# Attention into mixture of experts on one core: single steps of a written-out plan get offsets, work moves between VectorE and GpSimd, and all engines get a new order

## The chip, the cores and the metric

The kernel runs on one core of one Trainium2 chip. The metric is the device time of one execution in microseconds (us). PE is the matrix engine TensorE, DVE is VectorE, ACT is ScalarE, POOL is GpSimd, SP the engine that issues most DMAs.

## The reference

Inputs: q, k, v of 4 batches, 8 heads, 576 positions, 64 columns, and the weights of 8 experts. First an approximate attention with 32 landmarks a head, then an expert layer on its 2304 x 512 result.

```python
q_lm = q.reshape(B, H, m, S // m, D).mean(axis=3)        # m = 32, S // m = 18
k_lm = k.reshape(B, H, m, S // m, D).mean(axis=3)
A = sm(q, k_lm)                                          # sm: softmax of scaled products
Bm = sm(q_lm, k_lm)
C = sm(q_lm, k)
Z = Bm.transpose(0, 1, 3, 2) / (norm1 * norminf + 1e-06)
for _ in range(6):
    Z = 2 * Z - Z @ Bm @ Z
x = A @ Z @ C @ v
expert_idx = argmax(x @ w_gate); gate_w = softmax of it at that expert
h = maximum(x @ w1[e], 0); y = h @ w2[e]                 # each row by its own expert, up to a capacity
out = gate_w * y
```

## The kernel before

Heads are stacked on partitions in two groups of 64 columns. For each batch `b` the work is cut into streams, Python generators that yield one `Step` (an engine, a cost, what it depends on) ahead of the instructions that it issues:

- `loads`: q, k and v by DMA. `landmarks`: sums over 18 positions into `lmq` and `lmk`, in four pieces (q and k, each in two groups `g`). A letter in `CFG["lm"]` says who sums a piece: V is VectorE in one instruction, G is GpSimd in five (through `tr`), H is half and half.
- `chain`: Bm (`bp`), its softmax (`BB`), then `bbp` and six rounds `pp` on TensorE, each followed by an addition `PQ` on VectorE, and `Wd`. Batches 2 and 3 go through one chain together.
- `cpath` a = 0, 1: the products `psC` (256 and 320 columns), their maximum (L565), the bias (L567), the exponential `Cx` on ScalarE, the transposes `ctp` and `ctq`. `cval`: `cvp`, C times v.
- `apath` a = 0, 1: the products `psA`, then in `AW` a transpose, maximum, subtraction (L673), exponential, sum, product (L683) and a transpose into `AT` (L686). `CFG["aw"]` says whether VectorE or GpSimd does the subtraction and the product.
- `route`: `mtp` and its copy `MT` (what the expert layer needs of a batch), `gp`, `ltp`, `glg`; a copy `ei` of the expert's number goes to SP, which loads that expert's weights `w1` (four pieces, `w1load`) and `w2` (eight pieces, `wload`).

The expert layer assumes that a batch uses one expert and has a slow path, not run here, for the rest. A key is a batch's turn in it (0, 1, 2; on this path the last batch is written as zeros). The attention result isn't formed: `gps` is MT times w1, split in two parts `gh` and `gl` of reduced precision (L931, L933); A is split likewise into `ah` and `al` (L948, L951, engine by `CFG["al"]`). A hidden block is six products `hps` (L972) for one of 8 pieces `fc` of the hidden layer and one half `c` of the positions, then ScalarE and VectorE or GpSimd (by `CFG["rx"]`) turn it into `hx`. w2 is split into `wh` (ScalarE, L891) and `wl` (L897, VectorE or GpSimd by `CFG["lo"]`). An output tile is a sum over the 8 pieces, `ybank` or `yps` (L1031, L1036), scaled into `yo` and stored. Until the first output tile TensorE fills planned idle time with products of zeros (L1094).

`weave` is the planner, run when the program is built. It keeps a clock for each engine, takes from all ready steps those that could start soonest, and of those within a small window (`look`) the one with the lowest priority number. On TensorE a change of kind (reduced-precision blocks against the others) adds `sw` to the number. The order that comes out is each engine's program: every engine works its own list in order, and waits where something isn't there.

Of the kernel before, what the change touches and what calls it, by code (L numbers as in the profile page):

```python
# [14 lines left out]
ALU = mybir.AluOpType  # L15
# [3 lines left out]
class Step:  # L19
    def __init__(self, eng, cost, deps=(), order=(), name=None, res=None, nres=1, keep=False, free=None, prev=True, start=0, prio=None,  # L20
# [8 lines left out]
    sw=4000,  # L29
    sc='AAAV',  # L30
    rx='GGVVGVVVVVGGVGVGVGVVVGGGGGVGVGVGGGVVVGGVGVVGVVVG',
    look=0.05,
    tg='tfftfttffftfttfffffttfff',
    ce='AVAAAVAA',
    pa='ffsfffsf',
    aw='GVGGVGVVGVGGGGVV',
    ye='AAAVAAAAAVAVVAVA',
    lm='VVHVGGVVGVGGVVGV',
    al='VGGVVV',
    lo='VGVVGVVVGGGGGGGGGGGVVGVV',  # L40
    pr=[
# [4 lines left out]
    ],  # L46
    fr=[
        [2182, -3175, -6151, 655, -1689, 10070],
        [-3174, -3941, 2917, 6070, -3108, 5793],
        [-15, -4918, 3590, -371, -3463, -1305],  # L50
    ],
    sp=[-5732, -1101, 1345],
    ah=[-2564, -629, 3615, -5343, -3536, -3510],
    rl=[-3503, -3810, 5069],
    ev=[-3109, -45, -3647],
# [34 lines left out]
def weave(streams, banks, fill=None):  # L90
# [9 lines left out]
    def enable(s):  # L100
        step = s[2]
        for d in (*step.deps, *step.order):
            if d not in ev:
                wait.setdefault(d, []).append(s)
                return
        lag = step.start + HIN[step.eng]
        s[4] = max([0] + [ev[d] + lag for d in step.deps] + ([s[3] + lag] if step.prev and s[3] else []))
        s[5] = s[0] if step.prio is None else step.prio
        ready.append(s)

    def advance(s):
        s[2] = next(s[1], None)
        if s[2] is not None:
            enable(s)
        while spawned:
            advance([s[0], spawned.pop(0), None, s[3], 0, 0])

    for prio, gen in streams:
        advance([prio, gen, None, 0, 0, 0])
# [64 lines left out]
def nystrom_moe(ctx: ExitStack, tc: tile.TileContext, q, k, v, vtail, wgate, w1, w2, out, cap):  # L184
# [157 lines left out]
    def landmarks(b):  # L342
        lmt[b] = dict(q=None, k=None)
        for g in range(2):
            for nm in "qk":
# [9 lines left out]
                if e == "V":  # L355
                    parts = ((2, 3), (3, 4)) if b == 0 and g and nm == "k" else ((2 * g, 2 * g + 2),)
                    for i, (j0, j1) in enumerate(parts):
                        last = i + 1 == len(parts)
                        yield Step("V", 720 if j1 - j0 == 1 else 1290, deps=[f"ld{b}{nm}{j}" for j in range(j0, j1)], order=order,
                                   prev=False, name=f"lm{b}{g}{nm}" if last else None)  # L360
                        nc.vector.tensor_reduce(out=lm()[:, j0:j1, :], axis=AX.X, op=ALU.add,
                                                in_=st[b][nm][:, j0:j1, :].rearrange("p y (m t) -> p y m t", t=L))
                elif e == "P":
                    p = Step("P", 1450, deps=ld, order=order, prev=False, res="f", keep=True, kind="T")
# [3 lines left out]
                    for i in range(3):  # L368
                        if i:
                            yield Step("P", 1450, kind="T")  # L370
                        for t in range(6 * i, 6 * i + 6):
                            nc.tensor.matmul(ps, lhsT=ident, rhs=x[:, :, :, t], start=(t == 0), stop=(t == L - 1))
                    yield V(130, free=p, name=f"lm{b}{g}{nm}")
                    nc.vector.tensor_copy(lm()[:, 2 * g:2 * g + 2, :], ps)
                else:
                    j0, n = 2 * g, 2
                    if e == "H":
                        yield Step("V", 720, deps=ld[:1], order=order, prev=False, name=f"lv{b}{g}{nm}")
                        nc.vector.tensor_reduce(out=lm()[:, j0, :], axis=AX.X, op=ALU.add,
                                                in_=st[b][nm][:, j0, :].rearrange("p (m t) -> p m t", t=L))  # L380
                        j0, n = j0 + 1, 1
                    yield Step("G", 1300 if n == 2 else 700, deps=ld[2 - n:], order=order + ([f"lmg{b - 1}"] if b else []), prev=False)
# [55 lines left out]
    def V(c, **kw):  # L438
        return Step("V", c, **kw)

    def chain(*bs):
# [8 lines left out]
        def C(one, both):  # L450
            return both if two else one

        p = Step("P", C(222, 352), tag="a", deps=[x for b in bs for x in LM(b)],
# [54 lines left out]
        p = Step("P", C(356, 672), res="ch", keep=True)  # L508
# [10 lines left out]
        for it in range(6):  # L519
            last = it == 5  # L520
            p = Step("P", C(417, 770) if last else C(356, 672), res="ch", keep=True)
            yield p
            pp = pch.tile([128, n, 2, 32], F32, tag="ch", name="pp")
            for x in range(n):
                for j in range(4):
                    y = slice(32 * j, 32 * j + 32)
                    if last:
                        nc.tensor.matmul(pp[y, x, 1], lhsT=PQ[y, x, 0], rhs=PQ[y, x, 2], start=True, stop=False)
                        nc.tensor.matmul(pp[y, x, 1], lhsT=istk[y], rhs=PQ[y, x, 2], start=False, stop=True)
                    else:  # L530
                        nc.tensor.matmul(pp[y, x], lhsT=PQ[y, x, 0], rhs=PQ[y, x, 0:3:2], start=True, stop=True)  # L531
            if last:
                break
            yield V(C(200, 330), free=p)
            Pn = PQs[1 - it % 2][:, xs]
            nc.vector.tensor_tensor(Pn[:, :, 0:3:2, :], pp, PQ[:, :, 1:3, :], ALU.add)
            PQ = Pn
# [9 lines left out]
    def cpath(b, a):  # L547
# [18 lines left out]
        yield V(65)  # L566
        nc.vector.tensor_scalar(cs[:, 1, :, a], cs[:, 0, :, a], -SC1, None, op0=ALU.mult)  # L567
        Cx = at.tile([128, NG, n], F32, tag=f"C{a}", name="Cx")
        for x in range(NG):
            yield Step("A", 250 + n * 5 // 6, free=p if x else None, start=0 if x else 60,  # L570
                       name=[f"cx{b}{a}"] * x)
            nc.scalar.activation(Cx[:, x, :], t[:, x, :n], AF.Exp, bias=cs[:, 1, x, a:a + 1], scale=SC1,  # L572
                                 accum_out=sums[:, x, a:a + 1])
# [27 lines left out]
    def cjoin(b):  # L601
# [5 lines left out]
        yield Step("A", 300)  # L607
# [11 lines left out]
    def cval(b):  # L619
        for x in range(NG):  # L620
# [11 lines left out]
            def cvf(x=x, p=p, cvp=cvp):  # L632
                yield V(130, deps=[f"cg{b}"], order=[f"mt{b - 2}"] if b > 1 else ())
# [4 lines left out]
                yield V(130, free=p, name=[f"cv{b}{x}"] + [f"cv{b}"] * x)  # L638
                nc.vector.scalar_tensor_tensor(CV, cvp[:, 1, :], cf[:, 1, x, 1:2], CV, ALU.mult, ALU.add)
# [244 lines left out]
    def wsplit(b, key):  # L884
        st[b]["w"] = []
        for c in range(NFC):
# [12 lines left out]
            later(lo, e, 1280 if e == "G" else 610, name=f"ws{key}{c}", port=True)  # L899
# [268 lines left out]
```

## Time and profile before

| | |
|---|---|
| median of 3 runs | 188.54 us (187.79 to 188.80) |
| the profiled execution | 188.28 us |
| its span, first to last instruction | 186.6 us |
| busy: PE, DVE, ACT, POOL | 177.7, 108.2, 79.7, 78.6 us |

The span is what the profile shows; 1.68 us of the profiled execution lie around it. Instructions of different engines overlap, so busy times don't add up to the span.

### The profile page before, as it was taken

To read this page: it belongs to the slowest core of one execution; us is meant where nothing else is said; L and a number is where in the kernel's file an instruction comes from. 1 tells how busy PE (TensorE), PEld (TensorE's weight loads), DVE (VectorE), ACT (ScalarE), POOL (GpSimd) and SP (SyncE) were. 2 spreads that over 40 slices of the span, in tenths; PEclk is the share of its full clock that TensorE was granted. 3 is DMA by queue.
4 is the path that set the end of the run, shared out by engine and by line. 5 is a ranking of instruction groups with operands and counts; after the bars stand their busy time and mean duration, and the time that the engine had idled before them with its cause. 6 is when DMAs were issued, how large, how long until landed. Compare 5 with 4: busy or idle time off the path is not lost.

```text
span 186.6 us, 5484 instructions
## 1 busy us (share of the span) xinstructions
PE 177.7 (95%) x2191; PEld 136.0 (73%) x2199; DVE 108.2 (58%) x313; ACT 79.7 (43%) x202; POOL 78.6 (42%) x131
## 2 busy tenths in 40 slices
PE   7989987998999999999999999999999999999992
PEld 2435634667788788788778889688888899788891
DVE  2789999999899967884446767820002753211001
ACT  3026314976497402455496377501153976100020
POOL 7429996783037276505881256300025752100000
PEclk9999999999999999999999999999999999999998
DMA  5999969984631999284710059411115400011121
GB/s 187 401 407 405 378 233 349 335 287 134 218 134 21 394 366 359 75 265 166 226 56 4 4 180 362 137 32 56 56 56 154 134 0 0 4 32 56 63 84 41
DMA packets 17492, 31.95 MB, mean 171 GB/s; under 512 B 1520, under 2 KB 9584, under 8 KB 17456
## 3 DMA queue, kind: packets, MB, share of 16 engines
q1 hardware_dynamic: 17024, 31.07, 47.8%
q8 instruction: 19, 0.31, 0.7%
q10 hardware_dynamic: 432, 0.43, 0.7%
q14 instruction: 17, 0.14, 0.2%
HBM read 26.77 MB, written 4.72 MB: 169 GB/s over the span
## 4 chain that ended last, share of the span: by engine, by line
PE 71%; DVE 14%; DMA 6%; ACT 3%; issue 3%; POOL 2%; SPq 0%; DVEq 0%; ACTq 0%
PE yps L1031 19%; PE hps L972 17%; PE ybank L1031 16%; PE ybank L1036 6%; DMA qt<-in_q 3%; PE gps L691 3%; DMA w2t<-in_w 2%; PE pp L531 2%; DVE cs L565 2%; PE ctp L582 1%; PE cvp L629 1%; PE psC L559 1%; DVE gl L933 1%; PE psA L658 1%; ACT Cx L572 1%
## 5 line engine op out<-in xcount | busy, mean ns | idle before, releaser
L995 POOL TENSOR_TENSOR hx<-rr,hx 128x224 fp32r<-128x224 f32 (+2 forms) x38 | 22.3, 605 | 29.8 <-ACT hx L986 29.6
L1031 PE MATMUL yps<-wh,hx 128*128 128x512 f32 (+1 forms) x112 | 33.5, 375 | 0.0
L897 POOL TENSOR_TENSOR wl<-w2t,wh 128x512 fp32r<-128x512 f32 x14 | 17.8, 1286 | 31.6 <-ACT wh L891 30.0
L1031 PE MATMUL ybank<-wh,hx 128*128 128x512 f32 (+1 forms) x96 | 28.5, 371 | 0.0
L972 PE MATMUL hps<-ah,gh 128*128 128x288 f32 x80 | 25.2, 315 | 0.1
L1031 PEld LDWEIGHTS yps<-wh,hx 128*128 128x128 f32 x112 | 20.6, 188 | 4.2 <-issue 0.4
L972 PE MATMUL hps<-al,gh 128*128 128x288 f32 x80 | 23.6, 295 | 0.0
L972 PE MATMUL hps<-ah,gl 128*128 128x288 f32 x80 | 23.6, 295 | 0.0
L1031 PE MATMUL yps<-wl,hx 128*128 128x512 f32 (+1 forms) x56 | 21.0, 374 | 0.0
L1031 PEld LDWEIGHTS ybank<-wh,hx 128*128 128x128 f32 x96 | 17.6, 188 | 3.1
L891 ACT CAST wh<-w2t 128x512 fp32r<-128x512 f32 x24 | 14.8, 622 | 7.5 <-PE ybank L1031 3.9
L1031 PE MATMUL ybank<-wl,hx 128*128 128x512 f32 (+1 forms) x48 | 17.8, 371 | 0.0
L1094 PE MATMUL ybank<-wt 128*128 128x512 bf16 x58 | 15.7, 407 | 1.8 <-DVE wt L216 1.3
L1055 ACT ACTIVATE yo<-yps,fac 128x512 f32<-128x512 f32 (+1 forms) x5 | 3.2, 647 | 32.5 <-PE yps L1031 32.5
L972 PEld LDWEIGHTS hps<-ah,gh 128*128 128x128 f32 x80 | 15.0, 188 | 2.8 <-ACT BB L486 0.4
L997 DVE SCALAR_TENSOR_TENSOR hx<-hps,hx 128x288 fp32r<-128x288 f32 (+2 forms) x34 | 11.9, 374 | 7.5 <-ACT hx L989 7.3
L1057 DVE TENSOR_SCALAR yo<-ybank,fac 128x512 f32<-128x512 f32 x2 | 1.5, 752 | 24.7 <-PE ybank L1031 24.7
L972 PEld LDWEIGHTS hps<-al,gh 128*128 128x128 f32 x80 | 15.1, 188 | 0.0
L972 PEld LDWEIGHTS hps<-ah,gl 128*128 128x128 f32 x80 | 15.0, 188 | 0.0
L572 ACT ACTIVATE Cx<-psC,cs 128x256 f32<-128x256 f32 (+1 forms) x16 | 8.0, 499 | 15.6 <-DVE cs L567 15.4
L984 ACT ACTIVATE rr<-hps 128x288 f32<-128x288 f32 x23 | 9.5, 411 | 6.8 <-PE hps L972 6.6
L1094 PEld LDWEIGHTS <-wt 128*128 128x128 bf16 x65 | 6.1, 104 | 8.3 <-issue 2.8
(199 smaller groups left out, 355.4 us busy)
## 6 DMA issues: line engine op xcount, KB each, us to landing
w1t<-in_w SPq DMA_DIRECT2D x12, 512.0 KB, 5.8
w2t<-in_w SPq DMA_DIRECT2D x24, 256.0 KB, 5.0
qt<-in_q SPq DMA_DIRECT2D x8, 576.0 KB, 6.6
vm<-in_v SPq DMA_DIRECT2D x8, 512.0 KB, 7.0
kt<-in_k SPq DMA_DIRECT2D x7, 576.0 KB, 7.0
out<-yo SPq DMA_DIRECT2D x10, 256.0 KB, 2.5
out<-wt SPq DMA_DIRECT2D x4, 256.0 KB, 6.9
kt<-in_k SPq DMA_DIRECT2D x2, 288.0 KB, 6.9
```

The costliest lines, as they stand in the source:

```text
L531: nc.tensor.matmul(pp[y, x], lhsT=PQ[y, x, 0], rhs=PQ[y, x, 0:3:2], start=True, stop=True)
L572: nc.scalar.activation(Cx[:, x, :], t[:, x, :n], AF.Exp, bias=cs[:, 1, x, a:a + 1], scale=SC1, accum_out=sums[:, x, a:a + 1])
L691: nc.tensor.matmul(dsts[g][32 * c:32 * c + 32], lhsT=MT[64 * g:64 * g + 64, c, :], rhs=rhs[64 * g:64 * g + 64, c, :], start=True, stop=True)
L891: nc.scalar.copy(wh, w2t)
L897: (nc.gpsimd if e == "G" else nc.vector).tensor_tensor(wl, w2t, wh.bitcast(F32), ALU.subtract)
L972: nc.tensor.matmul(ps[:, :HS], lhsT=wt[:, g, fc % 2], rhs=a[:, g, ss], start=(n == 0), stop=(n == 3 * NG - 1))
L984: nc.scalar.activation(rr, ps[:, :HS], AF.Relu)
L995: nc.gpsimd.tensor_tensor(dst, rr[:, x0 - s0:x1 - s0], hi, ALU.subtract)
L997: nc.vector.scalar_tensor_tensor(dst, ps[:, x0 - s0:x1 - s0], 0.0, hi, ALU.max, ALU.subtract)
L1031: nc.tensor.matmul(ps[:, :dn], lhsT=hx[:, fc, o:o + 128], rhs=wt[:, d0:d1], start=(fc == seq[0] and o == t0 and wt is wh), stop=(fc == seq ...
L1036: nc.tensor.matmul(ps[:m], lhsT=hx[:, fc, t0:t0 + m], rhs=wt, start=(fc == seq[0] and wt is wh), stop=(fc == seq[-1] and wt is wh))
L1094: nc.tensor.matmul(ybank, lhsT=wt[:, 0:128], rhs=wt, start=True, stop=True)
```

## The change

The planner looks up an offset for each single step, by its stream and its place in it, and adds it to the priority. The stall for changing the kind of work on TensorE doubles, the window for choosing doubles, and several planned costs are set anew. The tables of engines and priorities are new. The factor -SC1 on the maxima of C is applied by ScalarE, no longer by VectorE. In a half-and-half landmark piece of k, GpSimd now takes the first half and VectorE the second; the pieces of batch 0 go V, V, V, H, where they went V, V, H, V. A variant of the chain by ScalarE (`ca`) is added, used only on the path that is not run.

```diff
-    sw=4000,
+    sw=8000,
-    rx='GGVVGVVVVVGGVGVGVGVVVGGGGGVGVGVGGGVVVGGVGVVGVVVG',
-    look=0.05,
+    rx='GGVVGGVVVVVVVGVGVGVVVVVGGGVVVGVGGGVVVGGVVVVGVVGG',
+    look=0.1,
...
-    aw='GVGGVGVVGVGGGGVV',
+    aw='GGGGGVVGVVGVGVVG',
...
-    lm='VVHVGGVVGVGGVVGV',
-    al='VGGVVV',
-    lo='VGVVGVVVGGGGGGGGGGGVVGVV',
+    lm='VVVHGGVVGVGGVVHV',
+    al='GGVVVV',
+    lo='VGGGVGGVVVGGVGGVVGVGVVVG',
...
-        s[5] = s[0] if step.prio is None else step.prio
+        s[5] = (s[0] if step.prio is None else step.prio) + CFG["off"].get(f"{s[6]}.{s[7]}", 0)
...
                     if e == "H":
-                        yield Step("V", 720, deps=ld[:1], order=order, prev=False, name=f"lv{b}{g}{nm}")
-                        nc.vector.tensor_reduce(out=lm()[:, j0, :], axis=AX.X, op=ALU.add,
-                                                in_=st[b][nm][:, j0, :].rearrange("p (m t) -> p m t", t=L))
-                        j0, n = j0 + 1, 1
...
+                        jv, j0 = (j0 + 1, j0) if nm == "k" else (j0, j0 + 1)
+                        n = 1
+                        yield Step("V", 720, deps=[f"ld{b}{nm}{jv}"], order=order, prev=False, name=f"lv{b}{g}{nm}")
+                        nc.vector.tensor_reduce(out=lm()[:, jv, :], axis=AX.X, op=ALU.add,
+                                                in_=st[b][nm][:, jv, :].rearrange("p (m t) -> p m t", t=L))
...
         nc.vector.tensor_reduce(out=cs[:, 0, :, a], in_=t[:, :, :n], axis=AX.X, op=ALU.max)
-        yield V(65)
-        nc.vector.tensor_scalar(cs[:, 1, :, a], cs[:, 0, :, a], -SC1, None, op0=ALU.mult)
+        yield Step("A", 130, start=60)
+        nc.scalar.mul(cs[:, 1, :, a], cs[:, 0, :, a], -SC1)
```

The order of the built programs shows what the tables do. First TensorE, in the chain of batches 2 and 3 (bbp, then pp; the numbers 156 and 157 are the two buffers of PQ). Before:

```order
L514 MATMUL bbp<-BB 32x64 x16
L559 MATMUL psC<-kt,lmq 32x256 x8
L972 MATMUL hps<-ah,gh 128x288
L972 MATMUL hps<-al,gh 128x288
...
L531 MATMUL pp<-PQ_156 32x64 x16
...
L531 MATMUL pp<-PQ_157 32x64 x16
L559 MATMUL psC<-kt,lmq 32x320 x8
L531 MATMUL pp<-PQ_156 32x64 x16
L582 MATMUL ctp<-ident,Cx 128x128 x4
```

TensorE's same place after the change:

```order
L539 MATMUL pp<-PQ_156 32x64 x16
L572 MATMUL psC<-kt,lmq 32x256 x8
...
L539 MATMUL pp<-PQ_157 32x64 x16
L1044 MATMUL ybank<-wh,hx 128x512
...
L539 MATMUL pp<-PQ_156 32x64 x16
L572 MATMUL psC<-kt,lmq 32x320 x8
L539 MATMUL pp<-PQ_157 32x64 x16
L595 MATMUL ctp<-ident,Cx 128x128 x4
L985 MATMUL hps<-ah,gh 128x288
```

Before, a hidden block of six stood alone between two steps of the chain, twice in this place; now the end of key 0's last output tile stands in one gap, psC and ctp in others, and the next hidden block begins a row of three. Through TensorE's whole order, unbroken runs of hidden and output products go from 20 to 14, and the products of zeros from 65 to 63.

Second GpSimd, from the second subtraction of the softmax of A in batch 0 on. Before:

```order
L673 TENSOR_TENSOR AW_167<-AW_167,amx 128x18x32
L385 TENSOR_TENSOR tr<-qt 128x576
...
L393 TENSOR_TENSOR lmq<-tr 128x64
L385 TENSOR_TENSOR tr<-qt 128x576
L683 TENSOR_TENSOR AW_167<-AW_167,amx 128x18x32
L387 TENSOR_TENSOR tr<-tr 128x64x4
L389 TENSOR_TENSOR tr<-tr 128x64x2
L391 TENSOR_TENSOR tr<-tr 128x64
L951 TENSOR_TENSOR al<-AT_122,ah 128x2x288
```

The same place of GpSimd after the change:

```order
L686 TENSOR_TENSOR AW_166<-AW_166,amx 128x18x32
L696 TENSOR_TENSOR AW_167<-AW_167,amx 128x18x32
L392 TENSOR_TENSOR tr<-qt 128x576
L394 TENSOR_TENSOR tr<-tr 128x64x4
L396 TENSOR_TENSOR tr<-tr 128x64x2
L964 TENSOR_TENSOR al<-AT_122,ah 128x2x288
L398 TENSOR_TENSOR tr<-tr 128x64
L400 TENSOR_TENSOR lmq<-tr 128x64
L696 TENSOR_TENSOR AW_166<-AW_166,amx 128x18x32
L910 TENSOR_TENSOR wl<-w2t,wh 128x512 x2
L964 TENSOR_TENSOR al<-AT_122,ah 128x2x288
```

Both products of the softmax and both al of batch 0 now stand on GpSimd, and two splits of w2 stand ahead of the second al, which belongs to the half that the first hidden blocks read (AW_166, a = 0).

Third SP, where it loads the weights of key 0. Before:

```order
L866 TENSOR_LOAD ei0_137
L866 ISA x2
L872 ISA
L872 DMA w1t_549<-in_w1 128x4x256
...
L881 DMA w2t_558<-in_w2 128x512
```

The same place of SP after the change:

```order
L879 TENSOR_LOAD ei0_137
L879 ISA x2
L894 ISA
L894 DMA w2t_480<-in_w2 128x512
...
L885 DMA w1t_519<-in_w1 128x4x256
```

Three pieces of w1 stood ahead of four of w2; now the four of w2 stand ahead of the w1.

## Rows read from the trace of the kernel before

**Rows 1.** The page: busy us, share of the span, instructions.

```profile
PE 177.7 (95%) x2191; PEld 136.0 (73%) x2199; DVE 108.2 (58%) x313; ACT 79.7 (43%) x202; POOL 78.6 (42%) x131
```

**Rows 2.** Stages: us, then busy PE, PEld, DVE, ACT, POOL, granted clock, DMA share, GB/s.

```profile
9.60:34.00 24.40, 21.53 (x451) 11.66 (x456) 22.88 (x66) 9.96 (x32) 17.75 (x27) 1.00 0.95 357
34.00:60.70 26.70, 25.81 (x469) 20.22 (x463) 24.88 (x77) 19.63 (x57) 13.74 (x20) 1.00 0.56 177
60.70:183.00 122.30, 122.08 (x1250) 100.72 (x1248) 54.65 (x150) 48.63 (x112) 40.99 (x49) 1.00 0.37 127
```

**Rows 3.** Chain of work that ended last: start us, us, engine, tile, line.

```profile
58.25 1.13 PE psA L658 x32
...
60.77 3.68 PE ybank L1036 x16
...
90.87 0.59 PE psC L559 x16
91.47 0.99 PE hps L972 x6
...
105.95 0.32 PE glg L718 x2
...
110.35 5.68 PE hps L972 x42
...
117.11 1.02 PE gps L691 x32
```

**Rows 4.** Timeline of PE: start us, us, instruction; in brackets the idle time before.

```profile
10.79 0.41 PE L559 MATMUL psC<-kt,lmq 64*32 64x256 f32 x2 [0.51 <-POOL lmq L393]
...
34.69 0.40 PE L972 MATMUL hps<-ah,gh 128*128 128x288 f32 x1
...
35.68 0.43 PE L514 MATMUL bbp<-BB 32*32 32x64 f32 x16
36.04 0.40 PE L972 MATMUL hps<-ah,gh 128*128 128x288 f32 x1
```

**Rows 5.** Timeline of POOL, 22 to 42 us.

```profile
22.93 1.16 POOL L673 TENSOR_TENSOR AW<-AW,amx 128x576 f32<-128x576 f32 x1
24.05 1.30 POOL L385 TENSOR_TENSOR tr<-qt 128x576 f32<-128x576 f32 x1
...
26.77 0.37 POOL L391 TENSOR_TENSOR tr<-tr 128x64 f32<-128x64 f32 x1
...
27.62 1.29 POOL L385 TENSOR_TENSOR tr<-qt 128x576 f32<-128x576 f32 x1
...
33.87 1.43 POOL L951 TENSOR_TENSOR al<-AT,ah 128x576 fp32r<-128x576 f32 x1 [0.78 <-DMA vm<-in_v]
...
41.29 1.28 POOL L897 TENSOR_TENSOR wl<-w2t,wh 128x512 fp32r<-128x512 f32 x1
```

**Rows 6.** Timelines of DVE and of ACT, 27 to 42 us.

```profile
27.85 1.08 DVE L567 TENSOR_SCALAR cs<-cs 128x2 f32<-128x2 f32 x1
...
31.70 0.76 DVE L686 STREAM_TRANSPOSE AT<-AW 128x576 f32<-128x576 f32 x1
...
41.46 1.12 DVE L611 TENSOR_TENSOR ce<-ce,cf 128x4 f32<-128x4 f32 x1
...
33.12 0.68 ACT L948 CAST ah<-AT 128x576 fp32r<-128x576 f32 x1
```

**Rows 7.** Timeline of SP from 20 us, and the view of tile w1t there.

```profile
23.48 1.73 SPq L872 DMA_DIRECT2D w1t<-in_w  x3
25.40 2.10 SPq L881 DMA_DIRECT2D w2t<-in_w  x4
...
DMA to landing us min/median/max: 3.6/6.0/8.9
```

**Rows 8.** The same two views from 105 us.

```profile
108.22 2.06 SPq L872 DMA_DIRECT2D w1t<-in_w  x3
...
DMA to landing us min/median/max: 3.4/4.5/6.5
```

More of the change, by code (lines that the diff above doesn't have):

```diff
@@ L112, in advance @@
         s[2] = next(s[1], None)
+        s[7] += 1
         if s[2] is not None:
             enable(s)
+        n = 0
         while spawned:
-            advance([s[0], spawned.pop(0), None, s[3], 0, 0])
-    for prio, gen in streams:
-        advance([prio, gen, None, 0, 0, 0])
+            advance([s[0], spawned.pop(0), None, s[3], 0, 0, f"{s[6]}.{s[7]}{'abcdefghijklmnop'[n]}", 0])
+            n += 1
+    for i, (prio, gen) in enumerate(streams):
+        advance([prio, gen, None, 0, 0, 0, str(i), 0])
     while ready:
@@ L354, in landmarks @@
                 e = CFG["lm"][4 * b + 2 * g + (nm == "k")]
-                if e == "V":
-                    parts = ((2, 3), (3, 4)) if b == 0 and g and nm == "k" else ((2 * g, 2 * g + 2),)
+                if e in "VW":
+                    parts = ((2 * g, 2 * g + 1), (2 * g + 1, 2 * g + 2)) if e == "W" or b == 0 and g and nm == "k" else ((2 * g, 2 * g + 2),)
                     for i, (j0, j1) in enumerate(parts):
                         last = i + 1 == len(parts)
-                        yield Step("V", 720 if j1 - j0 == 1 else 1290, deps=[f"ld{b}{nm}{j}" for j in range(j0, j1)], order=order,
+                        yield Step("V", 720 if j1 - j0 == 1 else 1260, deps=[f"ld{b}{nm}{j}" for j in range(j0, j1)], order=order,
                                    prev=False, name=f"lm{b}{g}{nm}" if last else None)
@@ L363, in landmarks @@
                 elif e == "P":
-                    p = Step("P", 1450, deps=ld, order=order, prev=False, res="f", keep=True, kind="T")
+                    p = Step("P", 725, deps=ld, order=order, prev=False, res="f", keep=True, kind="T")
                     yield p
@@ L367, in landmarks @@
                     x = st[b][nm][:, 2 * g:2 * g + 2, :].rearrange("p y (m t) -> p y m t", t=L)
-                    for i in range(3):
+                    for i in range(6):
                         if i:
-                            yield Step("P", 1450, kind="T")
-                        for t in range(6 * i, 6 * i + 6):
+                            yield Step("P", 725, kind="T", prev=False)
+                        for t in range(3 * i, 3 * i + 3):
                             nc.tensor.matmul(ps, lhsT=ident, rhs=x[:, :, :, t], start=(t == 0), stop=(t == L - 1))
@@ L520, in chain @@
             last = it == 5
[L521 removed]
+            e = CFG["ca"][bs[0]]
+            p = Step("P", C(417, 660) if last else C(356, 580) if e == "V" else C(520, 850), res="ch", keep=True)
             yield p
@@ L632, in cvf @@
             def cvf(x=x, p=p, cvp=cvp):
-                yield V(130, deps=[f"cg{b}"], order=[f"mt{b - 2}"] if b > 1 else ())
+                yield V(190, deps=[f"cg{b}"], order=[f"mt{b - 2}"] if b > 1 else ())
                 CV = sm.tile([128, D], F32, tag=f"CV{x}", name="CV")
@@ L897, in lo @@
                 (nc.gpsimd if e == "G" else nc.vector).tensor_tensor(wl, w2t, wh.bitcast(F32), ALU.subtract)
-            later(lo, e, 1280 if e == "G" else 610, name=f"ws{key}{c}", port=True)
+            later(lo, e, 1245 if e == "G" else 610, name=f"ws{key}{c}", port=True)
     def hidden(b):
```

50 lines of the change are left out of this document (29 added, 21 removed), and 8 rows, old and new, of the table pr.

## The prediction

> **What bounds the kernel now.** I read the page first. TensorE is busy 95% of the span, VectorE 58%, ScalarE 43%, GpSimd 42% [rows 1]. A share of that kind is an average over unlike stages, so the next view was the table of stages [rows 2]. From 60.70 to 183.00 us TensorE is busy 122.08 of 122.30 us: there the span is the sum of TensorE's own work, and a change can shorten it only by a cheaper order of that work. Before 60.70 it is not so. From 9.60 to 34.00 TensorE idles 2.9 us, and much of what it does there is filler (L1094); VectorE is busy 22.88 of 24.40 us, and from 34.00 to 60.70 24.88 of 26.70 us. So the front belongs to VectorE, helped by GpSimd (17.75 of 24.40 us). [...] The chain of waits says the same: hidden blocks (hps), then the first output tile at 60.77 us, and TensorE to the end [rows 3]. The question is therefore when the first output tile starts, how much real work is still left then, and what TensorE loses later.
>
> **The change, part by part.** The arithmetic stays; the multiplication of the C biases goes from VectorE to ScalarE, the rest is engine choice and order.
>
> *Where the first hidden block starts.* It was at 34.69 us [rows 4]. It needs both parts of the first half of A (ah, al), which come behind the second softmax product of batch 0. That product and its al now both stand on GpSimd, and the al behind two weight splits (wl). I walk GpSimd's queue. The second subtraction (L673) ends at 24.1 us [rows 5]; what stands ahead of it is about the same, except that the half sum there is now of the key piece that is loaded right behind the queries, so I take 24.2. Then: product of the other half 1.16 (25.4); three of five steps of a landmark sum, 24.05 to 26.77 in the rows, 2.7 (28.1); al 1.43 (29.5); the other two steps, 26.77 to 27.62, 0.85 (30.4); the second product 1.16 (31.5). VectorE's transpose of it takes 0.76 (32.3) and ScalarE's ah 0.68 (33.0) [rows 6]. Meanwhile GpSimd does two wl of 1.28 each (34.1), and al 1.43: 35.5. TensorE's own queue ahead of the block ends with psC, which waits until the split of the second gps has freed its bank; the same kind of adding along VectorE's queue brings it to 36.0. I take 36.0: **+1.3 us**. Bounds: 35.0 if ScalarE's splits come early and the two wl don't hold al, 38.5 if GpSimd is stretched (below).
>
> *What now stands ahead of it.* In the old order bbp of batch 1, two of its pp and psC of 256 columns stood behind the first hidden block, now ahead, in time in which TensorE was waiting. bbp took from 35.68 to 36.04 us, 0.36, pp has the same 16 products of 32x64 and is put at the same, and psC is 0.59 [rows 3, 4]: 0.36 x 3 + 0.59 = **-1.7 us**. One psA (half of the 1.13 us of two) [rows 3] and one ctp, put at about the same, go from ahead of the first output tile to behind it; they make that tile come earlier and the end not at all.
>
> *Fewer borders between kinds of work.* With `sw` doubled the plan keeps hidden and output blocks together. I counted their unbroken runs through the whole order of TensorE: 20 before, 14 now. A lone block of six takes 0.99 us, and 42 in a row take 5.68, so six of them 0.81 [rows 3]: a border costs 0.18, and six fewer give **-1.1 us**. The bounds are 0 (a block behind transposes shows no such loss) and 0.22 each.
>
> *Waits between the first hidden block and the first output tile.* TensorE idles 26.70 - 25.81 = 0.89 us there [rows 2]. VectorE loses work in this stretch: three of its six splits of the first w2 go to GpSimd, one al and one softmax product too, and the six bias products (one of 1.08 us [rows 6]). I take half: **-0.45 us**, bounds 0 and -0.9.
>
> *Filler.* 65 before, 63 now. It lies in time in which TensorE waits, so it is priced at nothing; if it were in the way, two of 512 columns are 0.5 us, at the 0.135 us that a product of 288 columns takes in the long row of 42 [rows 3].
>
> *New waits behind the first output tile.* In the old order, there are none. Batches 2 and 3 now have single steps of their chain between one psC or ctp of 0.6 us, where a hidden block of 0.99 stood; key 2's weights have less time (below). I put **+0.3**, bounds 0 and 1.5.
>
> *The queue of SP.* Key 0's first four pieces of w2 now stand ahead of w1. Requests of four w2 took 2.10 us [rows 7]. Batch 0's expert index comes earlier, since the al and the second product are out of VectorE's way, but nothing counts on it: even with the old request at 23.48, w1 is asked for at 25.6 and lands 3.6 to 8.9 us later, its median 6.0: 31.6, against a first gps that my walk has at 31.2. Its price is in the bound of 38.5, and zero in the sum.
>
> *Landmarks of batch 0.* VectorE sums both late query pieces and GpSimd one key piece. The first psC waits for queries only; it waited for GpSimd's sum to 10.79 us [rows 4] and now for VectorE's. That is up to 1 us earlier for C, and the keys' sum ends some 0.7 later for A. Both run into VectorE's full queue; I give it nothing beyond the walk.
>
> The sum: 1.3 - 1.7 - 1.1 - 0.45 + 0.3 = -1.65. The profiled execution took 188.28 us, its span 186.6 and 1.68 around it; the change brings 186.6. The median of the runs shown is 188.54, 0.26 above the profiled one, so I predict **186.9**.
>
> **A rule weighed.** One bias product on VectorE, two numbers a partition, took 1.08 us; it began at 27.85 and ended with GpSimd's sum, which ran from 27.62 to 28.91. The `ce` product at 41.46 took 1.12 and ended with GpSimd's wl of 41.29 to 42.57 [rows 5, 6]. So some instructions of VectorE stand still until GpSimd's is through. The other instructions of that size in the same stretch are a tenth as long, so the two cost some 2 us, and the first of them leaves VectorE. By these rows locks are part of the old time and the sum stays at 186.9. [...]
>
> **The rivals.**
>
> 1. *More than that.* GpSimd's queue is not what limits: first hidden block at 35.0, all 0.89 us of waits gone, nothing lost behind. 0.3 - 1.7 - 1.1 - 0.9 = -3.4: 185.1. For it speaks how much VectorE is relieved; against it the two wl ahead of al.
>
> 2. *Given back; no measurable change.* Key 2's first gps waits for w1. The path was: glg at 105.95, request at 108.22, the second piece asked for some 0.65 later, landing 4.5 (at most 6.5) later: 7.4 to 9.4 us. Between that glg and gps there were 11.2 us [rows 3, 8]; the new order puts 18 and 42 products of hps, mtp and gp between them: 2.4 + 5.7 + 0.4 + 0.3 = 8.8. So it holds by 1.4 or misses by 0.6. A miss, with w1 of key 0 late by 1 as above, leaves 188.5. For it speaks that all cover behind 60.70 us is TensorE's own work, which gets shorter; against it that the median landing holds.
>
> 3. *Slower, by locking.* The place is GpSimd's stretch from 24 to 36 us, with some 4 us more in it than before. Each VectorE instruction on the way to the second transpose that meets a GpSimd one waits up to 1.3 us. Two of full length beyond those of before cost 2.6 and bring 189.5, the point from which it is slower; three bring 190.8. [...]
>
> That the change does nothing is no case: the orders of all engines differ from the start.
>
> **How the numbers follow.** Forecast 185.9 to 187.6: 0.48. Rival 1, below 185.9: 0.12. Rival 2 and all that lies within 0.5% of 188.54, which is about what a measurement of this kernel can tell from no change (187.6 to 189.5): 0.25. Rival 3, above 189.5: 0.15. So faster 0.60, same 0.25, slower 0.15. The range must leave out no more than 0.2: from 184.9 (rival 1 with the border at 0.22) to 189.6, where the locks begin to count.
>
> **What would show it.** First hidden block near 36 us and first output tile near 58.5 (60.77 + 1.3 - 1.7 - 0.5 for three of the borders - 0.45 - 1.1 for the two moved steps gives 58.3). Hidden blocks in long rows without the 0.18. TensorE without idle time from there to the end; a wait before key 2's first gps would be rival 2; VectorE instructions of 1 us that should take 0.2, between 24 and 36 us, rival 3. The prediction is wrong if the first output tile comes at 60 us or later, or if TensorE idles more than 1.5 us behind it.

## The result, and the profile of the changed kernel

The changed kernel takes 189.75 us (median of five runs, 189.19 to 192.95; one disturbed run, the 192.95, is left out of the ratio), the kernel before 188.54. The ratio is 1.006, interval 1.0033 to 1.0088: 0.6% slower, where 0.9% faster was forecast. The profiled execution took 189.69 us, its span 187.9.

First the page's row of engines, then the table of stages (us, then busy time of PE, PEld, DVE, ACT, POOL, granted clock, DMA share, GB/s), cut at the first hidden block, the first output tile and TensorE's end. They answer to [rows 1, 2].

```profile
PE 178.6 (95%) x2196; PEld 135.1 (72%) x2197; DVE 112.6 (60%) x314; ACT 79.7 (42%) x205; POOL 70.1 (37%) x123
```

```profile
9.60:37.49 27.89, 25.81 (x539) 12.66 (x538) 25.08 (x75) 14.11 (x40) 21.99 (x29) 1.00 0.99 369
37.49:59.26 21.77, 21.65 (x369) 18.10 (x361) 16.50 (x51) 16.34 (x51) 14.12 (x20) 1.00 0.46 142
59.26:184.30 125.04, 122.83 (x1271) 101.04 (x1269) 64.75 (x168) 47.73 (x112) 27.99 (x40) 1.00 0.36 124
```

The first output tile came at 59.26 us, where its first product stood at 60.61 before. From there to the end TensorE needed 125.0 instead of 122.4 us, and idled 2.2 of them where it had idled 0.2 [rows 2]. So 1.35 us were won in front, and 2.7 lost behind.

The places are in TensorE's timeline. "issue" in the brackets means that no semaphore explains the idle time.

```profile
24.59 0.42 PE L468 MATMUL bp<-lmk,lmq 64*32 64x32 f32 x16
24.94 0.29 PE L539 MATMUL pp<-PQ 32*32 32x64 f32 x3
26.56 0.42 PE L539 MATMUL pp<-PQ 32*32 32x64 f32 x13 [1.33 <-issue]
...
75.80 1.10 PE L704 MATMUL gps<-w1t,MT 64*32 64x256 f32 x32 [0.19 <-PE psA L671]
...
93.26 0.65 PE L539 MATMUL pp<-PQ 32*32 32x64 f32 x32 [0.57 <-DVE PQ L547]
94.90 0.65 PE L539 MATMUL pp<-PQ 32*32 32x64 f32 x32 [0.30 <-DVE PQ L547]
...
103.98 0.44 PE L713 MATMUL mtp<-Wd,CV 128*64 128x128 f32 x4 [0.90 <-DVE Wd L554]
```

Two theories. **F**: the time is lost in front, at 25.0 us, where TensorE stops in the middle of 16 like products, three done and thirteen to do. **V**: it is lost behind the first output tile, at 93 and 95 us, where TensorE waits for PQ, which VectorE makes behind other work, and at 104, where it waits for Wd. A rival to V is that VectorE, 4.4 us busier than before, simply has too much to do. VectorE's timeline there, with one row of GpSimd's behind it:

```profile
89.51 0.42 DVE L547 TENSOR_TENSOR PQ<-pp,PQ 128x256 f32<-128x256 f32 x1
89.85 1.69 DVE L910 TENSOR_TENSOR wl<-w2t,wh 128x512 fp32r<-128x512 f32 x1
91.46 0.68 DVE L578 TENSOR_REDUCE cs<-psC 128x2 f32<-128x512 f32 x1
92.06 0.83 DVE L678 STREAM_TRANSPOSE AW<-psA 128x288 f32<-128x288 f32 x2
92.82 0.38 DVE L547 TENSOR_TENSOR PQ<-pp,PQ 128x256 f32<-128x256 f32 x1
93.13 0.73 DVE L683 TENSOR_REDUCE amx<-AW 128x18 f32<-128x576 f32 x1
93.79 0.73 DVE L1070 TENSOR_SCALAR yo<-ybank,fac 128x512 f32<-128x512 f32 x1
94.44 0.41 DVE L547 TENSOR_TENSOR PQ<-pp,PQ 128x256 f32<-128x256 f32 x1
...
100.93 0.42 DVE L554 TENSOR_TENSOR Wd<-pp,bmask 128x256 f32<-128x256 f32 x1
102.81 0.69 DVE L946 TENSOR_TENSOR gl<-gps,gh 128x512 fp32r<-128x512 f32 x1 [1.45 <-ACT gh L944]
103.42 0.41 DVE L554 TENSOR_TENSOR Wd<-pp,bmask 128x256 f32<-128x256 f32 x1
```

```profile
89.71 1.28 POOL L910 TENSOR_TENSOR wl<-w2t,wh 128x512 fp32r<-128x512 f32 x1 [1.12 <-ACT wh L904]
```

The second Wd could follow the first at 101.3 us and stands behind gl, which waits 1.45 us for ScalarE. The wl at 89.85 takes 1.69 us; another wl of VectorE, at 95.96, took 0.68. GpSimd had begun a wl 0.14 us earlier, which ended at 90.99; VectorE's ended at 91.54, 0.55 us behind it and 1.0 us later than its own 0.68 us would give. This is what the third rival calls a lock, but at 90 us, where the prediction did not look for it.

### The profile page after: what moved, and what is told of

Same layout as the page of the kernel before. It is cut to its first block, busy times and chain, and to the rows that moved or that the text cites. A ratio compares the mean times of both kernels' runs of the same rounds, so it can differ in the third digit from the quotient of the medians.

```text
span 187.9 us, 5472 instructions
## 1 busy us (share of the span) xinstructions
PE 178.6 (95%) x2196; PEld 135.1 (72%) x2197; DVE 112.6 (60%) x314; ACT 79.7 (42%) x205; POOL 70.1 (37%) x123
## 4 chain that ended last, share of the span: by engine, by line
PE 88%; DVE 6%; issue 3%; ACT 1%; DVEq 0%
PE hps L985 20%; PE yps L1044 19%; PE ybank L1044 15%; PE ybank L1107 9%; PE ybank L1049 6%; PE gps L704 3%; PE pp L539 3%; PE ctp L595 2%; PE psC L572 2%; PE psA L671 2%; PE cvp L642 2%; PE ltp L759 1%; DVE PQ L525 1%; PE bbp L521 1%; DVE hx L1010 1%
## 5 line engine op out<-in xcount | busy, mean ns | idle before, releaser
L1008 POOL TENSOR_TENSOR hx<-rr,hx 128x224 fp32r<-128x224 f32 (+2 forms) x32 | 17.9, 581 | 33.7 <-ACT hx L999 33.7
L910 POOL TENSOR_TENSOR wl<-w2t,wh 128x512 fp32r<-128x512 f32 x12 | 16.2, 1366 | 31.5 <-DVE wl L910 20.7
L985 PE MATMUL hps<-ah,gh 128*128 128x288 f32 x80 | 24.4, 306 | 0.1
L1107 PE MATMUL ybank<-wt 128*128 128x512 bf16 x63 | 18.3, 418 | 1.3 <-DVE wt L221 1.3
L1010 DVE SCALAR_TENSOR_TENSOR hx<-hps,hx 128x288 fp32r<-128x288 f32 (+2 forms) x40 | 13.8, 369 | 9.4 <-ACT hx L1002 9.0
L1068 ACT ACTIVATE yo<-yps,fac 128x512 f32<-128x512 f32 (+1 forms) x6 | 3.9, 653 | 35.1 <-PE yps L1044 35.1
L910 DVE TENSOR_TENSOR wl<-w2t,wh 128x512 fp32r<-128x512 f32 x12 | 9.6, 808 | 10.2 <-ACT wh L904 10.2
L1070 DVE TENSOR_SCALAR yo<-ybank,fac 128x512 f32<-128x512 f32 x4 | 3.0, 746 | 19.3 <-PE ybank L1044 17.2
L1002 ACT ACTIVATE hx<-hps 128x288 fp32r<-128x288 f32 x29 | 11.8, 415 | 3.7 <-PE hps L985 3.7
```

Of the source, the lines that this page charges most:

```text
L910: (nc.gpsimd if e == "G" else nc.vector).tensor_tensor(wl, w2t, wh.bitcast(F32), ALU.subtract)
L985: nc.tensor.matmul(ps[:, :HS], lhsT=wt[:, g, fc % 2], rhs=a[:, g, ss], start=(n == 0), stop=(n == 3 * NG - 1))
L1002: nc.scalar.activation(hx[:, fc, ss], ps[:, :HS], AF.Relu)
L1008: nc.gpsimd.tensor_tensor(dst, rr[:, x0 - s0:x1 - s0], hi, ALU.subtract)
L1010: nc.vector.scalar_tensor_tensor(dst, ps[:, x0 - s0:x1 - s0], 0.0, hi, ALU.max, ALU.subtract)
L1068: nc.scalar.activation(yo[:, d0:d1], ps[:, :d1 - d0], AF.Copy, scale=factor(t))
```

## The experiments

For all of them the planner's choice was first written out as a list, so that one step can be moved and no other follows. A step has a name of two numbers (stream and step); "x n" in the list is filler ahead of it. Their line numbers are 34 or more above those of the changed kernel (wl is L944, PQ L581, pp L573).

**Written out, unchanged.**

```diff
+    todo = [x.split("*") for x in PLAN.split()]
     while ready:
-        cand = {}
...
+        for x in todo:
+            s = by.get(x[0])
...
+            fill(int(x[1]))
```

> The changed kernel with its order written out as a list of steps instead of being chosen by the planner; every engine gets the same instructions in the same order. Theory V (the time was lost behind the first output tile, where VectorE has other work ahead of what TensorE waits for in the chain of batches 2 and 3: TensorE stood 0.57, 0.30, 0.90 and 0.18 us there): 189.2 to 190.2 us, the same four waits within 0.15 us. Theory F (the time was lost in front, in the stop of 1.33 us inside the products at 25.0 us that no semaphore explains, and which may or may not fall there in a given execution): if the stop is absent or shorter, the first hidden block starts up to 1.3 us before 37.5 and the time falls to 188.4.

Measured: ratio 1.0068 (1.004 to 1.0096), the same as the changed kernel's 1.006 within the intervals. The waits behind the first tile were 0.58, 0.30, 0.90, 0.18. The stop at 25 us was absent, with one of 0.41 at 44 us:

```profile
25.68 0.51 PE L573 MATMUL pp<-PQ 32*32 32x64 f32 x16
```

So V's waits recur and the stop comes and goes. F's forecast for a run without the stop, 188.4 us, failed: the profiled execution took 189.56 us and its span is 187.9 us, that of the first profile. The first bbp came at 18.01 us instead of 17.15, the first hidden block at 37.06 instead of 37.49.

**Steps of VectorE moved.** In the list, VectorE's steps alone (22.x are the chain's, 22.12 to 22.18 its PQ, 22.22 and 22.23 its Wd, 34.2 and 35.2 cs, 26.2 and 26.3 AW and amx):

```diff
 22.12
-49.6a.1
 34.2
...
-41.37a.1
 22.16
+41.37a.1
 35.2
 22.18
+49.6a.1
...
 22.22
-46.3a.2
 22.23
+46.3a.2
```

49.6a.1 is the wl, 41.37a.1 the yo, 46.3a.2 the gl. All three were moved in one kernel, the first two in another, gl alone in a third.

> Three VectorE steps of the changed kernel moved a few places back: a low part wl of key 1 and the scaling yo of output tile 4 behind the PQ steps that TensorE waits for, a low part gl behind both Wd. Theory V: the waits of 0.57, 0.30 and 0.90 us shrink to 0.2 or less together, PE's end moves from 184.3 to 182.5 to 182.9, and the time to 187.9 (187.5 to 188.4), a ratio to the kernel before of 0.997. The rival (the order only shifts a shortage of VectorE, which has 4.4 us more work than before, so the waits come back at later steps): 189.2 or more, with new VectorE waits of TensorE between 95 and 118 us that sum to over 1.2 us. Theory F: no change from 189.7, since the front stays.

> Only wl and yo moved behind the PQ steps. Theory V: the waits of 0.57 and 0.30 us at the 4th and 5th product go, that of 0.90 at the merge of the values (mtp, for Wd) stays or grows to at most 1.2 since its cause, gl behind ScalarE's gh, is untouched: 188.9 (188.5 to 189.3). The rival: 189.5 or more, mtp waits 1.6 us or longer.

> Only gl moved behind both Wd steps. Theory V: the 0.90 us at mtp goes to 0.1 or less, the two PQ waits stay 0.57 and 0.30: 188.9 (188.5 to 189.3). The rival: the later gl makes the next hidden blocks of key 1 or the logits wait 0.6 us or more, and the time stays over 189.5.

Measured: all three 1.0026 (0.9999 to 1.0054); wl and yo 1.0014 (0.9992 to 1.0036); gl 1.0066 (1.004 to 1.0092). The waits for PQ and for Wd went where their steps were moved, but gl alone gained nothing that the times show: the copy MT is then late behind gl, and the gate product gp waits 0.57 us for it. So wl and yo carry the gain. The forecast of 1.8 us for all three was too large: 0.8 came (1.0068 to 1.0026). The profiled execution of wl and yo was the slowest of its 13 (191.21 us, their median 189.22). It had stops without a semaphore at three places: 0.78 us at the 4th pp, and these two:

```profile
45.58 0.25 PE L676 MATMUL cvp<-vm,CT 128*32 128x64 f32 x2 [1.31 <-issue]
...
78.06 1.10 PE L738 MATMUL gps<-w1t,MT 64*32 64x256 f32 x32 [1.30 <-issue]
```

**Five moves.** MT (23.2) ahead of AW, and the yo of output tile 2 (41.29a.1), which waits for a free buffer, behind bst and BB (22.2, 22.3):

```diff
-41.29a.1
 22.2
 22.3
+41.29a.1
...
 26.7
+23.2
 26.8
...
-23.2
```

> The three moves of VectorE steps and two more: the copy of the merge product (MT) ahead of a scaling of the late queries (AW), and the scaling yo of output tile 2, which waits for a free buffer, behind the two steps of the border chain (bst, BB) that free TensorE's bank. Theory V: the waits of 0.57 us at gp and of 0.44 us at gps that the run with three moves still had go, TensorE needs 123.0 to 123.3 us from the first output tile to its end instead of 124.0, and the ratio to the kernel before goes from 1.0026 to 0.9975 (0.995 to 1.000). The rival (shortage of VectorE): ratio 1.001 or more, new waits for VectorE that sum to over 0.8 us.

Measured: 1.0009 (0.9981 to 1.0036), short of the forecast 0.9975; against the three moves (1.0026) the intervals overlap. In the profile the two more moves show: from the first output tile to the end it took 123.31 us, with three moves 124.00. Behind the tile 0.14, 0.13 and 0.28 us of waits are left, no shortage of VectorE. But the stop at 25 us was there with 1.05 us, and the kernel is only as fast as the one before.

**The order of SP's requests** (39.2 to 39.4 are w1, 42.1 to 42.4 are w2; the second kernel is the one before, with the edit reversed; a last one joins the first to the five moves).

```diff
-42.1 42.2 42.3 42.4
 39.2 39.3 39.4
+42.1 42.2 42.3 42.4
```

> The changed kernel with one edit: SP requests the four early pieces of w2 behind the first three of w1, as the kernel before does, instead of ahead of them. Theory F (the stops without a semaphore at 25 us come from TensorE's instructions waiting behind the loads that SP has requested by then): the stop at 25 to 26.6 us, which five executions of this order showed with 1.33, 0, 1.33, 0.78 and 0.35 us, is 0.3 us or less, the first hidden block starts 26.6 us after the first psC product instead of 27.7 on the mean, and the ratio to the kernel before is 1.002 to 1.004 instead of 1.0068. Theory V alone: the stop is what it was, the ratio 1.005 to 1.008, and the waits behind the first output tile are unchanged.

> The kernel before with the same edit the other way round: SP requests the four early pieces of w2 ahead of w1, some 4 us earlier. Theory F: stops without a semaphore of 0.3 to 1.3 us appear between 23 and 29 us, where the kernel before shows none over 0.16, and the ratio is 1.003 to 1.007. Theory V alone: no such stop, ratio 0.998 to 1.002, unless w1 comes late: its first piece would land at about 29 instead of 27.1 us and the first hidden block start after 34.7.

> The five moves on VectorE and w1 requested first, together. Theories V and F add up: ratio 0.994 (0.991 to 0.997), faster than both kernels. If only V holds: the same as the run with five moves within 0.0015. If neither: 1.002 or more.

Measured: 1.0307 (1.0266 to 1.0347), 1.0054 (1.0027 to 1.0082) and 1.0241 (1.0208 to 1.0273). F in this form fell. The stop at 25 us stayed (1.05 us in the first, 2.15 in the third). The kernel before got none; it got a wait of 1.10 us for w1 instead. Its profiled execution had a mean granted clock of 0.855, where the profile of the kernel before has 0.996, and took 16 gps products in 0.70 us instead of 0.67 and 16 psA products in 0.78 instead of 0.72; TensorE reaches each place later with it, so that half of the test is weak. The loss of some 5 us in the first is a different thing, seen on ScalarE and VectorE:

```profile
30.45 1.29 ACT L938 CAST wh<-w2t 128x512 fp32r<-128x512 f32 x2 [6.20 <-DMA w2t<-in_w]
31.65 0.67 ACT L995 CAST ah<-AT 128x576 fp32r<-128x576 f32 x1
32.23 0.25 ACT L515 ACTIVATE BB<-BB 128x64 f32<-128x64 f32 x1
```

```profile
32.51 0.22 DVE L517 TENSOR_REDUCE bst<-BB 128x2 f32<-128x66 f32 x1 [2.98 <-ACT BB L515]
```

In the new order ScalarE has two wh ahead of ah and BB. They wait for w2, and all that stands behind them waits too. The third run shows the same with 6.80 us. While TensorE waited its granted clock fell as well: 0.56 from 36 to 39 us in the first run, 0.50 from 30 to 33 us in the third. The early w2 is no choice of its own: the order needs it.

**The instruction stream shifted.** In the first six profiles of the changed order the stops over 0.3 us stood at the same three instructions: the 4th of 16 pp, the 70th of 80 cvp, the first gps. Tiny products on zeros at the start, in place of some of the 29 there, move all later instructions along the stream:

```diff
     def fill(n):
         if not st[0].get("y"):
+            if not st[0].get("tiny"):
+                st[0]["tiny"] = True
+                for _ in range(75):
+                    nc.tensor.matmul(ybank[:, 0:8], lhsT=wt[:, 0:128], rhs=wt[:, 0:8], start=True, stop=True)
+                n -= 11
             for _ in range(n):
```

75 for 11 shift by 64; 115 for 15 by 100; 104 for 14 by 90; 147 for 19 by 128.

> The run with five moves, with 11 of the 29 products on zeros at the start replaced by 75 tiny ones (8 columns), so that every later instruction of TensorE stands 64 products further on in its stream, and nothing else differs. The stops without a semaphore stood at the same three instructions in all executions of the changed order: the 4th of 16 pp products, the 70th of 80 cvp products, the first gps product of key 1. Theory F2 (they belong to places in the instruction stream, where TensorE has run to the end of what had been fetched): the first moves into the cvp products at 21 to 23 us, the other two go, and the ratio to the kernel before is 0.996 to 0.999 instead of 1.0009. If they belong to the work that stands there: same three places, ratio 0.999 to 1.003.

> The same with a shift of 100 products (115 tiny ones for 15 of the first 29). Theory F2: the stop in front moves to the products before that cvp group, at 20 to 22 us, the one at 44 us goes into the hidden blocks or gps before it and the one at 76 us into the output blocks, where one product takes 0.13 to 0.23 us, so both vanish; ratio 0.996 to 1.000. Otherwise as with 64.

> Five moves and a shift by 90 products. By the place in the stream the stop of 0.49 us that a shift of 100 showed at the 2nd of 24 hidden products moves 10 products on, to the 12th, behind 1.4 us of slow products, and is 0.2 us or less; in front the block's end falls among the 32 pp products at 27 us. Ratio 0.993 to 0.996. If the places do not follow: 0.996 or more, with the 0.49 us where it was.

> Five moves and a shift by 128 products, 256 instructions: the instruction queue of the profile moves packets of 16 KB. If TensorE's instructions come in pieces of 256, the stops stand at the same instructions as without a shift (4th of 16 pp, 70th of 80 cvp, first gps of key 1) and the ratio is 0.999 to 1.003. If the length is another, the stops stand elsewhere or are gone and the ratio can be 0.996 or less.

Measured, with the five moves each time: 1.0082 (1.0057 to 1.0107) for 64, 0.996 (0.9946 to 0.9974) for 100, 0.9962 (0.9942 to 0.9982) for 90, 1.0018 (0.9987 to 1.0048) for 128. The stops, in this order of shifts: 64, 100, 128.

```profile
26.91 0.45 PE L606 MATMUL psC<-kt,lmq 64*32 64x320 f32 x1
27.89 0.77 PE L606 MATMUL psC<-kt,lmq 64*32 64x320 f32 x15 [0.52 <-issue]
```

```profile
44.44 0.40 PE L1019 MATMUL hps<-ah,hx 128*128 128x288 f32 x1
45.33 0.29 PE L1019 MATMUL hps<-al,hx 128*128 128x288 f32 x1 [0.49 <-issue]
```

```profile
26.06 0.29 PE L573 MATMUL pp<-PQ 32*32 32x64 f32 x3
26.74 0.41 PE L573 MATMUL pp<-PQ 32*32 32x64 f32 x13 [0.38 <-issue]
```

With 128 the stop is back at the 4th pp. With 100 it is 28 products behind the 70th cvp, with 64 it is 64 behind the 4th pp: in these runs the places recur every 128 products, that is 256 instructions with their weight loads. From the 4th pp to the 70th cvp the traces have 381 weight loads, as many products go with them, and 6 instructions that only wait for a semaphore: 768, three times 256. The third place does not fit: from the 70th cvp to the first gps there are 327 products, 2.6 times 128.

Not as expected: with 64 the stop did not move back into the cvp products but on by 64, and the run was slower, not faster. Its profile has two more stops, 0.50 us at 89.83 and 0.28 at 95.20 us, 128 products apart, behind the first output tile; the timed runs were slower still than the profiled one (188.87 us, the fastest of six), which stays open. With 90 no stop over 0.3 us is left, as expected, but the time is no better than with 100, whose 0.49 us therefore cost nothing that the times show. These two are the fastest kernels of the study: 187.68 us against 188.6, and 188.06 against 188.66.

**Without the filler behind the stop** (five moves; 13 products on zeros between 27.5 and 36.2 us left out).

```diff
-2.21*2 3.2*3 12.9*2 40.1*4 3.6*2
+2.21 3.2 12.9 40.1 3.6
```

> The run with five moves without the 13 products on zeros between 27.5 and 36.2 us, which took 2.9 us of TensorE. If TensorE's own time bounds the way to the first hidden block: it starts at 36.3 instead of 37.5 us and the ratio goes from 1.0009 to 0.996. If the chain on VectorE and GpSimd behind the late stop bounds it (wl until 33.4, then al until 35.65): it starts at 37.0 or later, the removed time becomes waits for VectorE and GpSimd, and the ratio stays above 0.999.

Measured: 1.0041 (1.0013 to 1.007), first hidden block at 38.77 us. Waits for Wd, MT, Cx and PQ of 0.28, 0.72, 0.61, 0.40 and 0.42 us, 2.43 together, took the place of most of the 2.9 us of filler. From the end of the stop to the product gp it took 6.03 us, with the filler 6.36: up to there the chain on VectorE and ScalarE bounds the stretch, not TensorE. Behind it another thing happened, which neither forecast has. The stretches before and behind gp, in the columns of the table of stages, without the 13 products and then with them:

```profile
27.50:33.30 5.80, 3.80 (x108) 1.60 (x97) 5.56 (x23) 3.71 (x11) 5.65 (x6) 1.00 1.02 357
33.50:36.70 3.20, 3.20 (x46) 1.56 (x49) 2.36 (x5) 1.79 (x5) 2.35 (x2) 0.50 0.96 324
```

```profile
27.50:33.30 5.80, 5.42 (x109) 2.23 (x103) 5.46 (x21) 3.46 (x11) 5.66 (x6) 1.00 1.02 358
33.50:36.70 3.20, 3.00 (x71) 1.69 (x71) 3.09 (x6) 2.28 (x6) 2.44 (x2) 1.00 0.84 285
```

TensorE had been busy 3.80 of 5.80 us instead of 5.42, and its granted clock fell from 1.00 to 0.50; the 16 gps products there took 1.11 us instead of 0.66. That is why the first hidden block came later and not earlier. The time follows the clock too: the two of the twelve runs with a granted clock of 1.00 took 188.32 and 188.66 us, level with the kernel before, and the ten at 0.99 or less took 189.5 us and more. So in these runs this filler bought the clock, not nothing. The stop of the cvp products stood 13 products further on, as the stream says.

**Controls on the kernel before**: written out, and shifted by 100.

> The kernel before with its order written out, every engine's instructions unchanged: a second execution with a profile of the same program. Ratio 0.998 to 1.002. Theory F (the stops are a cost of the changed order): no stop over 0.3 us without a semaphore. If the kernel before has them as well: 0.3 to 1.3 us somewhere between 20 and 50 us in this execution, and the stops explain no part of the difference.

> The control: the kernel before with the same shift by 100 products. Two executions of it showed no stop over 0.16 us, so if the shift acts by the stops alone it has nothing to gain here: 0.9985 or more, and above 1.002 if block ends now fall where products are dense. If the tiny products gain by themselves: 0.994 to 0.997.

Measured: 1.0001 (0.9986 to 1.0016), no stop; and 1.0029 (1.0011 to 1.0048). The tiny products give nothing by themselves; here they cost 0.3%, and the profile of that run does not show where.

**The changed kernel, only shifted**, by 100 and by 90.

> The changed kernel, its order untouched, with only the shift by 100 products (115 tiny ones for 15 of the first 29 on zeros). If the stops and VectorE's order are two costs that add: 1.0019 (1.000 to 1.004) instead of 1.0068, with the waits of 0.57, 0.30 and 0.90 us behind the first output tile still there and no stop over 0.3 us at 26 us. If the shift gained only together with the moves: 1.005 or more.

> The changed kernel, its order untouched, with the shift by 90 products. If the stops cost it as much as they cost the run with five moves (0.4 to 0.5%): 1.002 (1.0005 to 1.004). If VectorE's order makes up nearly the whole loss, because TensorE after a stop would have waited for VectorE anyway: 1.0045 to 1.007. No stop over 0.3 us at 26 or 45 us in either case, and the waits of 0.57, 0.30 and 0.90 us unchanged.

Measured: 1.0057 (1.0034 to 1.008) and 0.9982 (0.996 to 1.0004). Neither fits two costs that add, and 0.9982 lies outside both forecasts. With 100 the stop at 26 us was gone, that at 45 us had 0.51 us, and the waits for PQ were there (0.61, 0.29). With 90 the stops and the waits for PQ were gone, although no step of VectorE had been moved; the wait of 0.90 us for Wd stayed. Its rows, VectorE's and GpSimd's:

```profile
89.48 0.68 DVE L944 TENSOR_TENSOR wl<-w2t,wh 128x512 fp32r<-128x512 f32 x1
```

```profile
89.51 1.79 POOL L944 TENSOR_TENSOR wl<-w2t,wh 128x512 fp32r<-128x512 f32 x1 [1.27 <-ACT wh L938]
```

Here VectorE's wl began 0.03 us ahead of GpSimd's, and GpSimd's took 1.79 us, where its next one, at 92.64 us, took 1.28. In the changed kernel, its replay, the run with gl and the shift by 100 VectorE's began 0.14, 0.12, 0.13 and 0.10 us behind and took 1.69 to 1.72. So in these five runs the two PQ waits, 0.87 us together, hang on which of two engines is first by a tenth of a microsecond.

## Why the prediction was wrong

The first bbp product came between 17.15 and 18.51 us in these executions, so the stages are compared from it on (us, worked out from the traces):

| kernel | stop at 25 to 28 us | first bbp to first hidden block | to first output tile | first tile to end | bbp to end |
|---|---|---|---|---|---|
| before; written out; shifted | 0; 0; 0 | 16.87; 16.86; 16.89 | 42.78; 42.50; 42.65 | 122.4 each | 165.2; 164.9; 165.0 |
| changed | 1.33 | 20.34 | 42.11 | 125.05 | 167.15 |
| changed, written out | 0 | 19.04 | 40.99 | 125.23 | 166.23 |
| changed, shift 100 | 0 | 19.02 | 40.95 | 124.71 | 165.65 |
| changed, shift 90 | 0 | 18.88 | 40.79 | 123.64 | 164.43 |
| five moves | 1.05 | 20.06 | 41.81 | 123.31 | 165.12 |
| five moves, shift 90 | 0 | 18.86 | 40.61 | 123.34 | 163.95 |

The step that failed is "New waits behind the first output tile": +0.3 was put there, with bounds 0 and 1.5, and 2.14 us came (0.19, 0.57, 0.30, 0.90, 0.18). Two causes are shown. One is the lock between the two wl, 0.87 us, undone by moving wl and in one run by 0.1 us of chance. The other is VectorE's strict order: gl, waiting for ScalarE, in front of Wd, 0.90 us. Moving gl alone only passed the wait on to MT; with MT moved too, 0.14, 0.13 and 0.28 us are left in the profile, and the times do not show this part by itself. The prediction's own mark, more than 1.5 us of idle time behind the tile, says the same. The argument "in the old order there are none" was about TensorE; nobody walked VectorE's queue at 90 and 103 us as GpSimd's was walked at 24 to 36.

The second miss is in front: the first hidden block came at 37.49 us instead of 36.0 and the first tile at 59.26 instead of 58.3. The replay, without the stop, had 37.06 and 59.00, so most of it is the walk to the first hidden block. Its end on GpSimd came out nearly right, al until 35.65 us where 35.5 was walked, but by luck: GpSimd began 1.4 us earlier than walked and then waited 1.15 us for TensorE and 0.85 for ScalarE. What held the block was TensorE's own queue ahead of it, the step that the prediction gave only as a result, "along VectorE's queue brings it to 36.0". ltp and psC came behind a PQ of VectorE that stands behind a landmark sum; in the run without filler the profile names that PQ as what ltp waits for:

```profile
34.62 1.34 DVE L366 TENSOR_REDUCE lmk<-kt 128x64 f32<-128x1152 f32 x1
35.88 0.28 DVE L547 TENSOR_TENSOR PQ<-pp,PQ 128x128 f32<-128x128 f32 x1
```

The stop of 1.33 us comes on top, and no step of the sum had a place for it. In the table it lengthens the way from bbp to the first hidden block by nearly its own length (18.9 to 19.0 without it, 20.06 with 1.05, 20.34 with 1.33). Counted from the span's start it costs less: in the profiles of this order with the early w2 and all its filler the block stood at 37.2 to 37.8 us with the stop at the 4th pp, and at 37.0 to 37.4 without a stop from 25 to 28 us. The stop ended at 26.2 to 26.7 us whether it was long or short, so what it took was in part only the lead of an early bbp.

Point by point:
- *First hidden block +1.3*: too small. Without the stop it is 2.0 to 2.2 us later, counted from bbp.
- *Waits between the first hidden block and the first output tile*: the -0.45 was too careful; 0.12 us of the 0.89 are left. From the block to the tile it took 21.8 to 21.9 us where the kernel before took 25.6 to 25.9, 3.7 to 4.2 less; the terms for that stretch (work moved ahead -1.7, psA and ctp -1.1, three borders -0.5, waits -0.45) say 3.75.
- *Work moved ahead and fewer borders*: the first tile should gain 2.3 us; without the stop it gains 1.6 to 2.0. Behind it, +1.1 for the moved psA and ctp and -0.5 for three borders say 0.6; 0.9 is left after the five moves, of which 0.55 are waits. The size of a border was not measured by itself.
- *w2 ahead of w1 at no cost*: right, and more than that: the new order needs it, the reverse costs 3%.
- *Filler at nothing*: with 63 of 65 left it holds, but the reason given, that it lies in time in which TensorE waits, leaves out the clock: without 13 of them the granted clock fell from 1.00 to 0.50.
- *Key 2's w1* (rival 2): no wait, gps began at 117.0 us.
- *Locking* (rival 3): right in kind and in the price of one lock (1.0 us), wrong in place; no lock of that size on the way from 24 to 36 us set the end. The 189.75 us lie in this rival's bracket by luck: it asked for two locks in front, and one came at 90 us.
- *C biases on ScalarE, landmarks*: not tried one by one; no wait of TensorE names them.

With the stops and most of the waits taken out the order is faster, as forecast, by less than half of the forecast: five moves and a shift by 90 stand 0.4% below the kernel before, where 0.9% was put. How the 0.6% of the changed kernel divides between stop and VectorE stays open, since the two meet: the shift by 90 also tips the lock (1.0068 to 0.9982), the shift by 100 does not (1.0057), and the five moves without a shift reach 1.0009.

## What to carry to other kernels

When an order changes, walk the queue of each helping engine at every place where the bound engine needs its result, all the way to the end of the span. Ask what stands ahead, what that waits for, and which instruction of another engine runs beside it: VectorE's wl took 1.69 us where it began 0.14 us behind GpSimd's, and 0.68 at 95.96 us. Where a matmul stream stops without a semaphore, always at one instruction, shift the stream by some tiny products at the start and time it, with several shifts: 90 and 100 gained 0.5% here, 64 lost 0.7%. Do so before judging an order by its time, since 10 products more or less took the same order from 0.6% slower to no difference. Before taking out products that only fill time, look at the granted clock behind them: here it fell from 1.00 to 0.50.

## What the runs showed of the hardware

Not expected: TensorE stops for 0.3 to 2.15 us in the middle of like products, in these runs at places that recur every 128 products (256 instructions with their weight loads). The profile of the changed kernel has a queue of kind "instruction" that moved 0.31 MB in 19 packets, 16 KB each:

```profile
q8 instruction: 19, 0.31, 0.7%
```

One of these packets ran from 23.89 to 24.94 us, ahead of the stop that ended at 26.56. The traces of all runs show the same: each of the 18 stops over 0.3 us inside pp, cvp, psC, psA or hps products ended 1.3 to 1.7 us behind the end of such a packet (worked out from the packets in the traces), short stops and long ones alike. That the next piece of the stream came late is the author's reading of these times; no run shows what the packets hold. What makes the stop 1.33 us in one execution and lets it stay out in the next was not found, and requesting w1 ahead of w2 did not change it. The stop ahead of the first gps does not fit: it is off the places, and where it had 0.34 to 1.30 us it ended 4.0 to 5.2 us behind the last packet. Its cause is open.

Also shown: of two wl that ran at once on VectorE and GpSimd, the one that began later was the long one. With the shift by 90, GpSimd's began 0.03 us later and took 1.79 us instead of 1.28; in the changed kernel VectorE's began 0.14 us later and took 1.69 instead of 0.68. And in the run without the 13 products TensorE's granted clock fell from 1.00 to 0.50 at 33.4 us behind a stretch in which TensorE was busy 3.80 of 5.80 us, and was 1.00 again from 37 us; with filler in that stretch, busy 5.42 of 5.80 us, it stayed at 1.00.
